# Two ordering edges in an interleaved attention and mixer kernel: the mixer's first loads and norm behind the attention's last steps, and the read-outs' denominators behind the row maxima of their step

## The chip, the cores and the metric

The kernel runs on one core of one Trainium2 chip. The metric is device time in microseconds (us) of one execution, so lower is better. One execution was also recorded by the hardware profiler; all rows of the profile and the trace come from that one.

## The reference

Four layers run one after the other on x, a sequence of S = 2048 rows with D = 640 columns: attention with a compressive memory, a gated mixer (gMLP), and both once more with the same weights.

```python
for i in range(2):
    x = x + A(layernorm(x))
    x = x + B(layernorm(x))

def A(x):                       # H = 32 heads of 20, N = 4 segments of 512 rows
    q, k, v = x @ wq, x @ wk, x @ wv        # per head and segment
    M, z = 0, 0
    for s in range(N):
        a_dot = softmax(q[s] @ k[s].T * 20**-0.5 + causal_mask) @ v[s]
        a_mem = (phi(q[s]) @ M) / (phi(q[s]) @ z + 1e-6)      # the memory's read-out
        o[s] = g * a_mem + (1 - g) * a_dot                    # g = sigmoid(beta), per head
        M += phi(k[s]).T @ v[s];  z += phi(k[s]).sum(rows)    # phi(t) = t + 1 if t > 0 else exp(t)
    return o @ wo

def B(x):
    z = gelu(x @ w_in)                      # 1728 columns: two halves of 864
    z1, z2 = z[:, :864], layernorm(z[:, 864:])
    return (z1 * (w_sp @ z2 + b_sp)) @ w_out
```

Products are made of fp16 parts: each operand is split into a high and a low half, and three matmuls (high by high, high by low, low by high) stand for one.

## The kernel before

**Stages.** Each attention is `phase1a` (class `Attention`, method `run`), each mixer is `phase1b` (output rows of the attention that are left, norm, product with w_in, gelu, norm of z2) and then `phase2` or `phase2s` (product with w_sp, gate, product with w_out). All in all: attention, mixer, attention, mixer.

**The attention's steps.** A segment has 16 pairs of heads, so there are N = 64 pairs in all four segments, and each pair takes three steps, c = 0, 1, 2. `run` counts steps t; pair n = t // 3 is the one whose exponentials are taken (`P`, L1276, on ScalarE). TensorE's order in this stage is the order of the program text (`manual_schedule` for PE); the other engines' order is made by a planner from priorities and from times that it simulates. In one step, in this order:

- `scores`: TensorE multiplies q by k for the row maxima of the pair two ahead (`mp`, L1267, then the mask, L1239), then k by q for the pair's own exponentials (`es`, the same lines). VectorE reduces `mp` to `mx` (L1283): 2 x 512 columns at c = 0, two blocks at c = 1, 2 x 256 at c = 2. ScalarE takes the exponentials.
- functions posted for this step by earlier ones (`post`, list `later`), the evictions of a read-out among them.
- `pvs` (L1320): 20 small matmuls for each head of a pair with `PH` and `PL`, the two halves of its exponentials, which ScalarE (L1293) and POOL (L1294; VectorE for some of the last four pairs) make.
- at c = 0, `maxes`: TensorE transposes the maxima of the next pair (`mtp`, L1301), ScalarE and VectorE split them (`mr`, L1303 and L1304), and two DMAs on the SP queue write them beside the pair's q (`qk<-mr`, L1306), where they act as the offset of the exponentials' argument.
- `until`: fill work for TensorE: the projections of q, k and v (`qps`, `kps`, `vps`), the output projection (`yps`, L1077) and, at steps given by a formula, a read-out.

**A read-out** is method `read`: for segments 1 to 3, and six of them per segment (five groups of heads, the last in two parts), TensorE multiplies phi(q) by the memory into `num` (L1163, L1167). Its function `out` is posted to the next step and has three VectorE instructions: `den` (L1172), its reciprocal (L1175) and the product `gm` (L1176). The read-out stands at the end of a step with c = 2, so `out` belongs to a step with c = 0. `num`, `mtp` and the products of a memory update (`mup`) are tiles of tag "ms" in pool `apm`, which has one buffer, one PSUM bank; the attention's PSUM pools use all eight banks, and `mp`, `es` and `pv` have one buffer each.

**Edges.** `tc.issue_after(i)` gives the instructions of its block that run on i's engine an edge: they are issued behind i. It adds no semaphore wait. `last_of` holds, for SP, ACT and DVE, the latest instruction of certain kinds: on SP a `qk` load or an `mr` DMA, on ACT an exponential or a v eviction, on DVE a row maximum `mx` or a v eviction. `hold` ties a block to all of them.

**The mixer's first tile.** `phase1b` goes over the 16 tiles of 128 rows in the order `ts`. Of tile 0 it loads the attention's result (`load`, L275), normalises it (`layernorm_stats`, L216 to L219, with POOL's power at L219; `xn`, L225), splits it (`xnhl`, L231 and L232) and transposes it by DMA into `th` (L233); TensorE then makes `zp` (L316) from `th` and w_in in two groups of 30 matmuls. The first such block, with the load of the second tile, stands in `tc.high_priority(offset=HP2)`, HP2 = 300:

```python
        with tc.high_priority(offset=HP2):
            a = load(ts[0])
            xn = attn_out(ts[0], *a)
            a = load(ts[1])
            th = xn_t(xn)
```

The rows that it loads (`x1_d`) are written in the course of the attention, the first of them long before its end, so nothing but buffers and priority holds the block back. In the trace its instructions stand at 616 to 635 us in the first attention's end, and at 1603 to 1617 and 1677 to 1688 us of the second, whose last row maximum is at 1802 us.

Of the kernel before, what the change touches and what calls it, by code (L numbers as in the profile page):

```python
# [2 lines left out]

# [32 lines left out]
HP2 = 300  # L36
# [209 lines left out]
NWO = 12  # L246


def phase1b(g, o_d, x, x1_d, z1_d, put, w0=None):
    nc, tc = g.nc, g.tc  # L250
    zs = ZS if w0 is None else ZB
    with ExitStack() as ctx:
# [50 lines left out]
        def xn_t(xn):  # L303
            th = pe2.tile([128, 2, KD, 128], F16, tag="th", name="th")
            hl = pe1.tile([128, 2, D], F16, tag="xnhl", name="xnhl")
            split_t(g, hl, th, xn)
            return th[:, 0], th[:, 1]
# [24 lines left out]

        g.mark = {}
        ts = [*range(NWO - 4), *range(NWO, NT), *range(NWO - 4, NWO)]
        with tc.high_priority(offset=HP2):
            a = load(ts[0])
            xn = attn_out(ts[0], *a)
            a = load(ts[1])
            th = xn_t(xn)
# [12 lines left out]
def whole(g, zh, zl):  # L352

    def put(t, z, pool):
        g.nc.scalar.copy(zh[:, t, :], z)
        g.nc.vector.tensor_tensor(zl[:, t, :], z, zh[:, t, :], ALU.subtract)

    return put


def blocks(g, zb):

    nc = g.nc
    even = {}

    def put(t, z, pool):
        j = t // 2
        l, r = z[:, :FHH], z[:, FHH:]

        def keep(b, src):  # L370
            nc.scalar.copy(zb[b][:, 0, j], src)
            nc.vector.tensor_tensor(zb[b][:, 1, j], src, zb[b][:, 0, j], ALU.subtract)

        def diff(a, b, nm):
            o = pool.tile([128, FHH], F32, tag=nm, name=nm)
            nc.gpsimd.tensor_tensor(o, a, b, ALU.subtract)
            return o

        if t % 2 == 0:
            keep(0, l)  # L380
            t1 = diff(r, l, "zt1")
            keep(3, t1)
            even[j] = r, t1
            return
        r0, t1 = even.pop(j)
        keep(1, l)
        keep(2, r)
        t2 = diff(r, t1, "zt2")
        keep(4, t2)
        keep(5, diff(r, r0, "zt3"))  # L390
        keep(6, diff(l, t2, "zt1"))

    return put
# [463 lines left out]
class Attention:  # L857
# [34 lines left out]
    def hold(self):  # L892
# [3 lines left out]
            held.enter_context(self.tc.issue_after(i))  # L896
        return held

    def soon(self, f):

        if self.now is None or self.now < 0:
            f()
        else:
            self.post(1, f)
# [240 lines left out]
    def read(self, s, m, c0):  # L1145

        g, nc = self.g, self.nc
        heads = UH[m]
        nh = len(heads)
        mst = self.mst[s % 2]  # L1150
        for i in range(max(m - 1, 0), m + 1):
            assert self.held["q", i] == s and self.held[s % 2, i] == s, (s, m, i, self.held)
        self.readout.add((s, m))
        if c0 == 0:
            self.gm[s, m] = self.pl2.tile([128, 4, 8, DH], F32, tag="gm", name="gm")
        gm = self.gm[s, m]
        n = min(6, nh - c0)
        f = heads[c0] - TH[m][0]
        low = [h for h in TH[m - 1] if h in heads[c0:c0 + n]] if m else []
        tp = self.pm.tile([128, L], F32, tag="ms", name="num")[:, :4 * n * (DH + 1)].rearrange("p (t h d) -> p t h d", t=4, h=n)  # L1160
        for t in range(4):
            c = slice(128 * t, 128 * t + 128)
            nc.tensor.matmul(tp[:, t], self.phq[m][:, c], mst[:, m, f:f + n, :], start=True, stop=not low,  # L1163
                             skip_group_check=True)
            if low:
                fl, nl = low[0] - TH[m - 1][0], len(low)
                nc.tensor.matmul(tp[:, t, :nl], self.phq[m - 1][:, c], mst[:, m - 1, fl:fl + nl, :],  # L1167
                                 start=False, stop=True, skip_group_check=True)

        def out():  # L1170
            den = self.u2.tile([128, 4, 6], F32, tag="den", name="den")[:, :, :n]
            nc.vector.scalar_tensor_tensor(den, tp[:, :, :, DH], g.epsd,  # L1172
                                           g.gate[:, heads[c0]:heads[c0] + n].unsqueeze(1).to_broadcast((128, 4, n)),
                                           ALU.add, ALU.mult)
            nc.vector.reciprocal(den, den)  # L1175
            nc.vector.tensor_tensor(gm[:, :, c0:c0 + n, :], tp[:, :, :, 0:DH],  # L1176
                                    den.unsqueeze(3).to_broadcast((128, 4, n, DH)), ALU.mult)

        self.post(1, out)

    def update(self, s, m, pk):

# [172 lines left out]
    def run(self, nseg=NSEG):  # L1355
        pairs = [(s, m, h0) for s in range(nseg) for m in range(NU) for h0 in UH[m][::2]]
        N = self.N = len(pairs)
# [42 lines left out]
        for c in order:  # L1400
            w = V if c[0] in "vp" else U
            beg = step(acc)
            if c[0] in "vp":
                i = int(c[1:])
# [9 lines left out]
            else:  # L1414
                s, m = int(c[0]), int(c[1])
                it = self.unit(s, m)
                i = NU * s + m - 4
# [39 lines left out]
        g = self.g  # L1457
# [14 lines left out]
            self.later[3 * i - LEAD + 2] = [lambda w=w: self.update(*w)]  # L1472
        for t in range(-LEAD, END):
            self.now = t
            f, c = divmod(t + self.LF, 3)
            if c == 0 and 0 <= f + self.LM < N:
                self.fetch(f + self.LM)
            p, r = divmod(t - self.LV - 2, 3)
            if r == 0 and 0 <= p < N:
                self.combine(p, *pairs[p])  # L1480
            n, c = divmod(t, 3)
            self.scores(n, c)
            for f in self.later.pop(t, ()):
                f()
            for h in range(2):
                p, r = divmod(t - self.LV - h, 3)
                if r == 0 and 0 <= p < N:
                    for _ in self.pvs(p, h, *pairs[p]):
                        pass
                if h == 1 and c == 0 and 0 <= n - 1 + self.LM < N:  # L1490
                    self.maxes(n - 1 + self.LM)
                if r == 0 and 0 <= p + 1 < N:
                    self.cast(p + 1, h)
            until(t + 1)
# [6 lines left out]
def phase1a(g, a, top, nseg=NSEG):  # L1501
    a.top = top
    with ExitStack() as ctx:
        a.setup(ctx)
        ctx.enter_context(g.tc.manual_schedule(engines=ENGINES))
        a.run(nseg)


@with_exitstack
def interleaved_layers(ctx, tc, x, wq, wk, wv, wo, beta, w_in, w_sp, b_sp, w_out, out):  # L1510
    nc = tc.nc
    g = Ctx()
    g.nc, g.tc = nc, tc
    cp = consts(g, ctx)
    g.bsp = cp.tile([128, NT], F32, tag="bsp", name="bsp")
    g.wpw = cp.tile([128, NT], F32, tag="wpw", name="wpw")
    g.wiv = cp.tile([128, NT], F32, tag="wiv", name="wiv")
    attn_consts(g, cp, beta)
    ats = ExitStack()
    attn_weights(g, ats, wv, wq, wk, wo, w_in, w_out)  # L1520

    def dram(name, shape, dt=F32):
        return nc.dram_tensor(name, shape, dt, kind="Internal").ap()

    def rows(a):
        return [a[0, t * 128:(t + 1) * 128, :] for t in range(NT)]

    g.st = [dram(f"st{i}", (D, 3, 2, L), F16) for i in range(2)]
    g.turned = [[dram(f"turned{t}_{i}", (128, 2048), F16) for i in range(2)] for t in range(NT)]
    kept = kept_tiles(g, ats)  # L1530
    xs = [rows(x), [dram(f"x2_{t}", (128, D)) for t in range(NT)], rows(out)]
    x1_d = [[dram(f"x1_{i}_{t}", (128, D)) for t in range(NT)] for i in range(2)]
    o_d = [[dram(f"o{i}_{n}", (L, 2, D), F16) for n in range(NSEG)] for i in range(2)]
    att = [Attention(g, xs[i], o_d[i], x1_d[i], kept) for i in range(2)]
    att[0].b_sp = b_sp
    for i in range(2):
        z1_d = [dram(f"z1_{i}_{t}", (128, FH)) for t in range(NT)]
        with ExitStack() as zs:
            with ExitStack() as top:
                phase1a(g, att[i], top)  # L1540
                if i:
                    ats.close()
                    w0 = zs.enter_context(tc.tile_pool(name="w0", bufs=1, reuse_waits="tile")).tile([128, 2, 7 * D], F16, name="w0")
                zp = zs.enter_context(tc.tile_pool(name="z2", bufs=1, reuse_waits="tile"))
                if i:
                    zb = [zp.tile([128, 2, NT // 2, FHH], F16, name=f"zb{j}") for j in range(7)]
                    phase1b(g, o_d[i], xs[i], x1_d[i], z1_d, blocks(g, zb), w0)
                else:
                    zh = zp.tile([128, NT, FH], F16, name="zh")
                    zl = zp.tile([128, NT, FH], F16, name="zl")  # L1550
                    phase1b(g, o_d[i], xs[i], x1_d[i], z1_d, whole(g, zh, zl))
            if i:
                phase2s(g, w_sp, x1_d[i], z1_d, zb, w0, xs[i + 1])
            else:
                phase2(g, w_sp, x1_d[i], z1_d, zh, zl, xs[i + 1], att[1])
# [26 lines left out]
```

## Time and profile before

| | us |
|---|---|
| runs (3), median | 2359.9 |
| runs, lowest and highest | 2358.45, 2361.67 |
| the profiled execution | 2362.26 |
| its span, first to last instruction | 2360.5 |
| first to last exponential of the first attention | 112.9 to 646.7 |
| first to last exponential of the second attention | 1314.4 to 1817.3 |
| mean granted TensorE clock | 0.977 |

The profiled execution lies 2.4 us above the median of the runs and 0.6 us above the slowest. In the profile PE is TensorE's matmul, PEld its weight load, DVE VectorE, ACT ScalarE, SP the queue that issues the DMAs. A row of the timeline has start, length, engine, line, operation, the tiles written and read, the shape, how many instructions are merged, and in brackets the idle time before it with what ended it. A row of stretches has the stretch, its length, the busy us of PE, PEld, DVE, ACT and POOL with the number of instructions, the granted clock (1.00 is full speed), the DMA engines' share and GB/s.

### The profile page before, as it was taken

To read this page: it belongs to the slowest core of one execution; us is meant where nothing else is said; L and a number is where in the kernel's file an instruction comes from. 1 tells how busy PE (TensorE), PEld (TensorE's weight loads), DVE (VectorE), ACT (ScalarE), POOL (GpSimd) and SP (SyncE) were. 2 spreads that over 40 slices of the span, in tenths; PEclk is the share of its full clock that TensorE was granted. 3 is DMA by queue.
4 is the path that set the end of the run, shared out by engine and by line. 5 is a ranking of instruction groups with operands and counts; after the bars stand their busy time and mean duration, and the time that the engine had idled before them with its cause. 6 is when DMAs were issued, how large, how long until landed. Compare 5 with 4: busy or idle time off the path is not lost. (4 is left out here: it accounts for less than half of the span.)

```text
span 2360.5 us, 50370 instructions
## 1 busy us (share of the span) xinstructions
PE 2184.8 (93%) x20490; PEld 1302.3 (55%) x20490; DVE 1503.1 (64%) x2790; ACT 1171.3 (50%) x1452; POOL 973.1 (41%) x726
## 2 busy tenths in 40 slices
PE   4778889899899999988998888999999999999998
PEld 2445555566645555555554555656566555555655
DVE  7578868777754543444533688787776668546454
ACT  3279678777732331111212697887776334322321
POOL 2078678888720100000001688888787323000000
PEclk9999899999999999999999999999999999999999
DMA  5553545555553457766665336454453634877885
GB/s 160 158 148 98 128 108 131 119 146 133 140 177 94 124 172 198 212 185 193 180 152 140 85 93 172 104 134 101 124 166 108 146 87 112 247 210 193 216 215 126
DMA packets 509416, 350.14 MB, mean 148 GB/s; under 512 B 409280, under 2 KB 444224, under 8 KB 504064
## 3 DMA queue, kind: packets, MB, share of 16 engines
q1 hardware_dynamic: 509184, 346.93, 55.7%
q8 instruction: 160, 2.62, 0.5%
q14 instruction: 72, 0.59, 0.1%
HBM read 160.83 MB, written 97.93 MB: 110 GB/s over the span
## 5 line engine op out<-in xcount | busy, mean ns | idle before, releaser
L1294 POOL TENSOR_TENSOR PL<-P,PH 128x1280 f16<-128x1280 f32 x248 | 649.9, 2622 | 121.8 <-ACT PH L1293 109.2
L1283 DVE TENSOR_REDUCE mx<-mp 128x2 f32<-128x1024 f32 (+3 forms) x512 | 408.9, 817 | 106.6 <-PE mp L1239 104.9
L1276 ACT ACTIVATE P<-es,sc 128x1024 f32<-128x1024 f32 (+1 forms) x384 | 370.4, 965 | 145.1 <-PE es L1239 142.6
L1293 ACT CAST PH<-P 128x1280 f16<-128x1280 f32 x256 | 320.4, 1253 | 19.8 <-PE pv L1320 11.5
L219 POOL TENSOR_TENSOR lnrs<-lnve,mhalf 128x1 f32<-128x1 f32 x92 | 56.6, 624 | 598.7 <-DVE lnve L218 595.4
L316 PEld LDWEIGHTS <-th 128*128 128x128 f16 x1920 | 188.1, 98 | 171.5 <-issue 8.6
L668 PE MATMUL gp<-zh,wt 128*128 128x432 f16 x1024 | 231.2, 346 | 0.0
L668 PEld LDWEIGHTS <-wt 128*128 128x128 f16 x1536 | 150.3, 98 | 128.9
L1267 PEld LDWEIGHTS <-qk 60*128 60x128 f16 (+1 forms) x2048 | 91.4, 94 | 227.8 <-issue 156.9
L469 PEld LDWEIGHTS <-wt 128*128 128x128 f16 x1344 | 131.5, 98 | 112.6
L1267 PE MATMUL mp<-qk 60*128 60x512 f16 (+3 forms) x1024 | 138.7, 308 | 40.2 <-DVE mx L1283 39.1
L1267 PE MATMUL es<-qk 64*128 64x512 f16 (+3 forms) x1024 | 136.2, 302 | 37.5 <-ACT P L1276 26.4
L1239 PEld LDWEIGHTS <-big 64*128 64x128 f16 x3072 | 142.0, 96 | 51.6 <-issue 4.9
L1320 PE MATMUL pv<-vs,PH 128*128 128x41 f16 x2560 | 167.9, 183 | 2.1 <-DVE ab L1336 2.0
L1044 PE MATMUL vps<-wvh,xt 128*128 128x320 f16 x640 | 155.1, 309 | 13.6 <-DMA xt<-xnhl 11.9
L1320 PE MATMUL pv<-vs,PL 128*128 128x41 f16 x2560 | 164.0, 182 | 1.6 <-POOL PL L1294 1.6
L1320 PEld LDWEIGHTS <-PH 128*128 128x128 f16 x2560 | 142.7, 96 | 18.8
L316 PE MATMUL zp<-wi1h,th 128*128 128x432 f16 x640 | 148.2, 346 | 0.6 <-DMA th<-xnhl 0.6
L1320 PEld LDWEIGHTS <-PL 128*128 128x128 f16 x2560 | 143.5, 97 | 4.3 <-POOL PL L1294 2.1
L668 PE MATMUL gp<-zl,wt 128*128 128x432 f16 x512 | 135.3, 346 | 0.0
L639 DVE TENSOR_REDUCE am<-wr 128x1 f32<-128x2048 f32 x16 | 36.5, 2284 | 152.1 <-DMA wr<-in_B_w_sp_dram 152.1
L1101 PE MATMUL kps<-xt,wkh 128*128 128x512 f16 x380 | 123.4, 394 | 6.2 <-DVE phl L1135 6.1
(248 smaller groups left out, 4384.6 us busy)
## 6 DMA issues: line engine op xcount, KB each, us to landing
wr<-in_B_w_sp_dram SPq DMA_DIRECT2D x32, 1024.0 KB
qk<-st SPq DMA_DIRECT2D x256, 120.0 KB
x<-x SPq DMA_DIRECT2D x56, 320.0 KB
z<-z SPq DMA_DIRECT2D x32, 432.0 KB
cz<-z SPq DMA_DIRECT2D x32, 432.0 KB
turned<-wt SPq DMA_DIRECT2D x24, 512.0 KB
wt<-turned SPq DMA_DIRECT2D x24, 512.0 KB
st<-qhl SPq DMA_DIRECT2D x40, 256.0 KB
```

The costliest lines, as they stand in the source:

```text
L316: nc.tensor.matmul(zp[:, n, :FHH], a[:, k, :], b[:, k, c:c + FHH], start=(k == 0 and j == 0), stop=(k == KD - 1 and j == 2))
L469: nc.tensor.matmul(o[:, :FHH], wt[:, x, m, :], zb[b][:, y, m, :], start=start and i == j == 0, stop=i == NP - 1 and j == 2, skip_group_che ...
L668: nc.tensor.matmul(gp[:, n, :FHH], ready[t][:, k % 2, a, k // 2, :], b[:, k, n * FHH:(n + 1) * FHH], start=(i == 0 and j == 0), stop=(i == ...
L1044: nc.tensor.matmul(ps, a[:, k, c], b[:, k, n * 320:(n + 1) * 320], start=(i == 0), stop=(i == 14))
L1101: nc.tensor.matmul(ps, a[:, k, c], b[:, k, :], start=(i == 0), stop=(i == 14))
L1239: nc.tensor.matmul(out, g.big[r, 64 - 64 * s:192 - 64 * s], mk, start=False, stop=s == 1, skip_group_check=True)
L1267: nc.tensor.matmul(out[:, h, o:o + w], a[r, ac], b[r, bc], start=o == 0, stop=False, skip_group_check=True)
L1276: self.last_of["ACT"] = nc.scalar.activation(P[:, :, 512 * c:512 * c + ew], es[:, :, :ew], AF.Exp, scale=g.esc).ins
L1283: self.last_of["DVE"] = nc.vector.tensor_reduce(self.mx[m][:, :, i], mp[:, :, o:o + w], AX.X, ALU.max).ins
L1293: nc.scalar.copy(PH, P[:, h])
L1294: (nc.gpsimd if h == 0 or n < self.N - self.TAIL else nc.vector).tensor_tensor(PL, P[:, h], PH, ALU.subtract)
L1320: nc.tensor.matmul(pv[:, i, h, :], x[:, c:c + 128], v[:, j, h0 + h, :], start=(j == 0 and x is PH), stop=(j == i and x is PL), skip_group_ ...
```

## The change

`phase1b` gets the context for its first block from outside: `Attention.ended`, which keeps the high priority and adds an edge to each instruction of `end_of`. That list is taken from `last_of` at the start of step 3N - 4 = 188: the last `mr` DMA on SP (step 186), the last row maximum on DVE (step 185) and the exponential of step 187 on ACT. And a read-out's `out` is wrapped in an edge to `last_of["DVE"]`: it runs in the step after the products, behind `scores`, so that this is the row maximum of that step.

```diff
-def phase1b(g, o_d, x, x1_d, z1_d, put, w0=None):
+def phase1b(g, o_d, x, x1_d, z1_d, put, first, w0=None):
...
         ts = [*range(NWO - 4), *range(NWO, NT), *range(NWO - 4, NWO)]
-        with tc.high_priority(offset=HP2):
+        with first:
             a = load(ts[0])
             xn = attn_out(ts[0], *a)
             a = load(ts[1])
...
+    @contextmanager
+    def ended(self):
+
+        with self.tc.high_priority(offset=HP2), ExitStack() as held:
+            for i in self.end_of:
+                held.enter_context(self.tc.issue_after(i))
+            yield
...
             nc.vector.tensor_tensor(gm[:, :, c0:c0 + n, :], tp[:, :, :, 0:DH],
                                     den.unsqueeze(3).to_broadcast((128, 4, n, DH)), ALU.mult)
 
-        self.post(1, out)
+        def held():
+            with self.tc.issue_after(self.last_of["DVE"]):
+                out()
+
+        self.post(1, held)
...
         for t in range(-LEAD, END):
             self.now = t
+            if t == 3 * N - 4:
+                self.first, self.end_of = self.ended(), [*self.last_of.values()]
...
-                    phase1b(g, o_d[i], xs[i], x1_d[i], z1_d, blocks(g, zb), w0)
+                    phase1b(g, o_d[i], xs[i], x1_d[i], z1_d, blocks(g, zb), att[i].first, w0)
...
-                    phase1b(g, o_d[i], xs[i], x1_d[i], z1_d, whole(g, zh, zl))
+                    phase1b(g, o_d[i], xs[i], x1_d[i], z1_d, whole(g, zh, zl), att[i].first)
```

More of the change, by code (lines that the diff above doesn't have):

```diff
@@ L1 @@
-from contextlib import ExitStack
+from contextlib import ExitStack, contextmanager
 from itertools import islice
```

## The prediction

> **What bounds the kernel now.** I read the page first, then stretches of equal work in both attentions, then single read-outs. Section 1 of the page gives busy time, share of the span and instructions of each engine:
>
> ```profile
> PE 2184.8 (93%) x20490; PEld 1302.3 (55%) x20490; DVE 1503.1 (64%) x2790; ACT 1171.3 (50%) x1452; POOL 973.1 (41%) x726
> ```
>
> TensorE leads, but the change touches only the two attentions, so their stages decide. In the view of stretches each row gives the length and the busy us of PE, PEld, DVE, ACT and POOL with instruction counts, then the granted clock, DMA share and GB/s. Rows come in pairs: the same steps of the first and of the second attention, cut at starts of the exponentials.
>
> ```profile
> 508.27:530.18 21.91, 21.66 (x301) 13.18 (x300) 16.30 (x34) 17.41 (x22) 18.47 (x13) 1.00 0.46 122
> 1672.87:1700.92 28.05, 24.61 (x301) 14.05 (x300) 20.37 (x40) 18.16 (x23) 19.03 (x14) 0.88 0.46 120
> 530.18:569.32 39.14, 39.12 (x537) 24.07 (x534) 28.68 (x58) 30.98 (x40) 33.15 (x22) 1.00 0.55 137
> 1700.92:1740.06 39.14, 39.11 (x537) 24.07 (x534) 28.67 (x58) 30.97 (x39) 33.15 (x22) 1.00 0.60 151
> 616.78:634.98 18.20, 13.94 (x211) 9.48 (x208) 15.79 (x32) 12.61 (x15) 12.51 (x11) 1.00 0.58 172
> 1789.81:1805.55 15.74, 13.66 (x211) 9.22 (x208) 10.86 (x20) 11.16 (x13) 12.24 (x9) 1.00 0.29 89
> ```
>
> Two things stand here. Undisturbed, the attention is TensorE's own pace (39.12 busy of 39.14). And lost time stays lost: the second attention loses 6.14 us in the second row (28.05 - 21.91), and the 39.14 us that follow are as long as in the first attention, where nothing had been lost. So a stall of TensorE is priced in full where it is saturated.
>
> **Part one: the denominators.** A read-out's products (`num`, on TensorE) end a step; its three VectorE operations (`den`, reciprocal, `gm`) belong to the next step. That next step always has c = 0, since read-outs stand at t = 2 (mod 3); it begins with `mp`, whose 1024 columns per partition VectorE reduces to `mx`, and after the pv products it has the transpose `mtp` of `maxes`. `num` and `mtp` share the one buffer of tag "ms". Here is a typical one, VectorE's timeline (start, length), then TensorE's:
>
> ```profile
> 537.80 0.24 DVE L1172 SCALAR_TENSOR_TENSOR den<-num,sc,gate 128x24 f32<-128x24 f32 x1 [1.89 <-PE num L1167]
> 538.07 0.30 DVE L1175 RECIPROCAL den<-den 128x24 f32<-128x24 f32 x1
> 538.48 0.66 DVE L1176 TENSOR_TENSOR gm<-num,den 128x480 f32<-128x480 f32 x1
> 539.05 1.22 DVE L1283 TENSOR_REDUCE mx<-mp 128x2 f32<-128x1024 f32 x1
> 540.19 0.68 DVE L1118 SCALAR_TENSOR_TENSOR qhl<-qps,qhl 128x512 f16<-128x512 f32 x1
> ```
>
> ```profile
> 538.35 0.25 PE L1239 MATMUL mp<-maskq,big 64*128 64x128 f16 x4
> ...
> 539.33 0.18 PE L1320 MATMUL pv<-vs,PL 128*128 128x41 f16 x1
> 539.35 0.27 PE L1301 MATMUL mtp<-ident,mx 128*8 128x128 f32 x1
> ```
>
> Today `gm` is done at 539.14, before `mtp` wants the buffer, and it lies beside `mp` on TensorE: it costs nothing. Behind `mx` that cover is gone, and `mtp` waits for it. That the dependency exists, and what it does when it bites, the trace shows. First the read-outs' tiles and `mtp`'s own row of semaphore waits, then the one place where `mtp` was late for it, and the delay from `mp` to `mx` on an idle VectorE:
>
> ```profile
> L1172 DVE SCALAR_TENSOR_TENSOR den<-num,sc,gate x36: 218/243/244, 224.5 to 1788.6; 128x24 f32<-128x24 f32 x30, 128x8 f32<-128x8 f32 x6
> ...
>   PE num L1167: 26.1, 15
>   PE num L1163: 7.8, 9
> who waited for it (us, times):
>   PE mtp L1301: 2.0, 2
> ```
>
> ```profile
> L1301 PEldq EVENT_SEMAPHORE  x36: 51/51/51, 225.8 to 1789.7; - x36
> ```
>
> ```profile
> 1680.21 0.89 DVE L216 BATCH_NORM_STATS2 lnst<-x 128x6 f32<-128x320 f32 x2 [2.31 <-DMA x<-x]
> ...
> 1682.12 0.66 DVE L1176 TENSOR_TENSOR gm<-num,den 128x480 f32<-128x480 f32 x1
> ```
>
> ```profile
> 1682.92 0.27 PE L1301 MATMUL mtp<-ident,mx 128*8 128x128 f32 x1 [1.57 <-DVE gm L1176]
> ```
>
> ```profile
> 1676.91 0.25 PE L1239 MATMUL mp<-maskq,big 64*128 64x128 f16 x4
> ```
>
> ```profile
> 1677.20 0.69 DVE L1283 TENSOR_REDUCE mx<-mp 128x2 f32<-128x512 f32 x1 [1.60 <-PE mp L1239]
> ```
>
> There are 36 read-outs, 30 wide and 6 narrow, and `mtp` carries 36 extra semaphore waits. The new moment of `mtp` at the typical place: `mp` ends at 538.60; `mx` starts 0.04 later (1677.20 against 1676.91 + 0.25); VectorE issues the next one 1.14 after that (539.05 to 540.19); `den` to the end of `gm` takes 1.34 (537.80 to 539.14); `mtp` follows 0.14 behind (1682.78 to 1682.92). Sum 2.66, so 541.26 instead of 539.35: **1.91 us of TensorE idle**. Queued behind `mtp` are the projection matmuls and the next step's `mp` and `es`, hence the exponentials. The narrow ones have a shorter chain:
>
> ```profile
> 615.60 0.23 DVE L1172 SCALAR_TENSOR_TENSOR den<-num,sc,gate 128x8 f32<-128x8 f32 x1 [0.86 <-PE num L1163]
> ...
> 616.42 1.23 DVE L1283 TENSOR_REDUCE mx<-mp 128x2 f32<-128x1024 f32 x1
> ```
>
> 0.82 in place of 1.34, so 1.39 us each. Before 24 of the 36 VectorE stood idle for `num` (15 + 9 above): it is free there, the typical case. At two thirds of each kind that is 20 x 1.91 + 4 x 1.39 = 43.8 us. At the other 12 VectorE comes late already, some of `mtp`'s wait exists, and the new part lies between 0 and 1.91; I take two thirds, 1.3 each, since only two of them show a wait of `mtp`: 15.6. Together **+59 us** (bounds 44 and 30 x 1.91 + 6 x 1.39 = 66). `mx` itself comes 0.41 earlier (538.64 for 539.05), worth nothing while `mtp` ends last.
>
> How much comes back later? Between the first and the last read-out of each attention TensorE is not saturated everywhere:
>
> ```profile
> 224.49:617.12 392.63, 360.75 (x4902) 231.67 (x4900) 303.99 (x596) 297.38 (x378) 314.67 (x217) 0.96 0.50 128
> 1415.55:1790.15 374.60, 352.77 (x4899) 225.55 (x4897) 293.01 (x583) 289.78 (x365) 314.16 (x219) 0.98 0.52 135
> ```
>
> Idle: 31.9 and 21.8, 54 us. Waits for an engine with a backlog would shrink when that engine gets 1.9 us to catch up; round trips through one buffer would not. I take a seventh: **-8** (0 to -27).
>
> **The clock.** The next rows are stretches of 3.41 us, cut where the granted clock changes, each with the one after it:
>
> ```profile
> 1321.62:1325.03 3.41, 1.63 (x21) 1.08 (x21) 2.32 (x6) 2.90 (x5) 3.41 (x2) 1.00 0.99 127
> 1325.03:1328.44 3.41, 3.41 (x56) 2.53 (x55) 1.87 (x7) 1.79 (x3) 2.15 (x2) 1.00 0.27 73
> 1680.02:1683.43 3.41, 1.59 (x29) 1.14 (x30) 3.02 (x8) 1.11 (x1) 1.83 (x2) 1.00 0.16 47
> 1683.43:1686.84 3.41, 2.04 (x10) 0.77 (x10) 3.38 (x5) 1.73 (x2) 1.30 (x1) 0.51 0.00 0
> ```
>
> Idle of 1.78 in a stretch left the clock at 1.00, idle of 1.82 was followed by 0.51. A wide stall leaves TensorE idle from 539.51 (end of pv) to 541.26, 1.75 us: just under, and over it with any other gap in the same stretch. If stretches run on regardless of the work, a stall lies wholly in one with chance (3.41 - 1.75) / 3.41 = 0.49; I let half of those reach the limit: 30 x 0.49 / 2 = 7, each costing half of 3.41: **+12** (0 to 61, all 36). [...]
>
> **Part two: loads and norm of phase1b's first tile.** The norm that now stands in the second attention's middle blocks VectorE on a load (the 2.31 at 1680.21); moved to the end, its 6.14 us go. In the first attention it costs 18.20 - 15.74 = 2.46. A second such norm lies in the second attention; between 0 and 6.14, I take 1, since one load was seen blocking. **-9.6**.
>
> What it costs at the end: moved are two loads on SP and, of the first tile, two statistics, aggregate and variance on VectorE, POOL's power, `xn`, ScalarE's copy, VectorE's low half and the transposing DMA; the second tile follows its load. SP must first issue the last `mr`, VectorE the last `mx`, ScalarE an exponential. Queued behind the statistics are then `rs`, `ab` and the PL subtractions of the last pairs, for which the pv products wait: a load waited for there like the one of 2.31 is in the upper bound.
>
> ```profile
> 1677.30 0.34 SPq L275 DMA_DIRECT2D x<-x  x1
> ...
> 1687.24 1.37 SPq L233 DMA_TRANSPOSE th<-xnhl  x1
> ```
>
> ```profile
> 1809.88 0.50 SPq L1306 DMA_DIRECT2D qk<-mr  x1
> ```
>
> ```profile
> 1824.92 0.17 DVE L1331 TENSOR_TENSOR rs<-pv,iomg 128x8 f32<-128x8 f32 x1 [1.59 <-PE pv L1320]
> ```
>
> ```profile
> 1827.49 7.00 PE L316 MATMUL zp<-w,th 128*128 128x432 f16 x30 [2.62 <-DVE ab L1336]
> ```
>
> The load goes out at 1810.4; the transposing DMA follows a load by 9.9 us (1677.30 to 1687.24) and issues for 1.4: `th` is there at about 1822 or later, and the first `zp` group can stand behind the last pv products (1824.9) instead of before them. A group takes up to 7.0, so the second group starts near 1831 instead of 1827.5; TensorE no longer waits for `ab`, which gives some back. I take 3.5 for both attentions (0 to 10). **Part two: -6** (-10 to +4).
>
> **Sum:** 59 - 8 + 12 - 6 = +57. The profiled execution took 2362.3 us (span 2360.5); the median of the runs is 2359.9. From the median: **2417**. How the planner reorders other queues no trace of before shows; I allow 6 us either way.
>
> **Rivals.** [...] (2) Every stall halves it: 59 - 8 + 61 - 6 = +106, 2466. For it: 0.51 after 1.82; against: stalls cut by a border. (3) Half of the stalls is taken back where TensorE idles anyway: 59 / 2 - 6 = +24, 2384. For it: 54 us of idle; against: 39.12 of 39.14. (4) The other side: the stall is covered. Place: the step behind each read-out; if `mp` there waits for `mx` and not for TensorE's own work, the chain through `mx` paces it, and 0.41 earlier gives 30 x 0.41 = 12 us: -12 - 6, 2342. It decides from the point where TensorE has over 1.91 us idle behind each read-out; the saturated rows say it has 0.02 in 39.14. (5) The tie changes nothing, because VectorE's order comes out as before: -6, 2354; the `last_of` of that step is the `mx` of its own c = 0, so I see no way to it but an oversight.
>
> **Numbers.** Forecast 0.48, (1) 0.20, (2) 0.10, (3) 0.11, (4) 0.06, (5) 0.04, no change 0.01. What this kernel's measurement can tell from no change is about 0.2%, 4.7 us. Faster: (4) and (5), 0.10; same 0.01; slower 0.89. The range 2378 to 2442 holds the forecast with its bounds, (1), most of (3) and the lower part of (2); outside are (4), (5) and some 0.08.
>
> **What would show it.** Right: `mtp` waiting for `gm` some 30 times, 45 to 65 us in all; `mx` ahead of `den` at every read-out; the pair at 1672.87 as long as its twin plus one stall; stretches at granted clock 0.5 behind some stalls; no norm of phase1b in the second attention's middle. Wrong: those waits absent, or present while the steps' lengths stay.

## The result and the profile after

The changed kernel takes **2446.4 us** (median of 4 runs, 2445.05 to 2448.38) against 2360.8 us (4 runs, 2358.45 to 2362.92) for the kernel before on the same chip: a ratio of 1.0371, 95% interval 1.0355 to 1.0387, or +85.6 us. Forecast were +57 and a range up to 2442. The sign and the mechanism hold; the size does not, and rows show which terms were too small. The profiled execution took 2445.05 us (span 2443.3).

TensorE's semaphore waits in the trace of the changed kernel (us in total, times, longest):

```profile
PE mtp L1313 <- DVE gm L1184: 71.9, 36, 4.5
PE zp L316 <- DMA th<-xnhl: 7.4, 3, 3.6
```

The first row stood at 2.0 us and 2 times before. All 36 read-outs now hold `mtp`. The second row stood at 0.6 us and once before; its growth belongs to part two.

The stretches of the prediction, at the same steps, in the changed kernel; the last two rows are the steps t = 45 to 186 of the two attentions:

```profile
522.56:546.77 24.21, 21.71 (x300) 13.08 (x299) 16.16 (x33) 17.71 (x23) 18.50 (x13) 1.00 0.40 110
1737.88:1762.10 24.22, 21.73 (x301) 13.10 (x299) 16.18 (x33) 17.72 (x22) 18.50 (x13) 1.00 0.39 108
546.77:597.64 50.87, 43.59 (x534) 25.46 (x531) 28.41 (x58) 31.41 (x39) 33.33 (x23) 0.90 0.41 106
1762.10:1812.45 50.35, 43.57 (x541) 25.47 (x537) 28.55 (x58) 31.33 (x39) 33.09 (x22) 0.90 0.50 140
223.33:668.87 445.54, 385.01 (x5077) 241.39 (x5074) 313.01 (x615) 311.43 (x389) 326.36 (x225) 0.94 0.44 115
1454.05:1881.62 427.57, 375.41 (x5075) 236.90 (x5072) 293.83 (x590) 302.46 (x375) 322.62 (x225) 0.96 0.44 116
```

The same steps before:

```profile
225.74:634.98 409.24, 373.10 (x5078) 240.24 (x5075) 318.30 (x625) 309.17 (x391) 326.15 (x227) 0.96 0.51 130
1416.80:1805.55 388.75, 364.84 (x5075) 233.85 (x5072) 302.39 (x600) 300.12 (x376) 325.36 (x227) 0.98 0.51 133
```

Three things are to be seen. The norm is gone from the second attention's middle: 28.05 and 21.91 us have become 24.22 and 24.21. The saturated stretch of 39.14 us has become 50.87, and only part of that is idle: TensorE's idle there is 50.87 - 43.59 = 7.3 us, but its *busy* time has grown from 39.12 to 43.59 for the same matmuls, at a granted clock of 0.90. Over all these steps the time grows by 75.1 us: idle from 60.1 to 112.7 (+52.6), busy from 737.9 to 760.4 (+22.5). Nearly all of the busy part is the clock, as the records of the clock show below.

**The typical stall** came out as worked out. VectorE, then TensorE, in the changed kernel:

```profile
613.04 1.23 DVE L1295 TENSOR_REDUCE mx<-mp 128x2 f32<-128x1024 f32 x1 [2.73 <-PE mp L1251]
614.18 0.23 DVE L1180 SCALAR_TENSOR_TENSOR den<-num,sc,gate 128x24 f32<-128x24 f32 x1
...
614.45 0.30 DVE L1183 RECIPROCAL den<-den 128x24 f32<-128x24 f32 x1
...
614.85 0.66 DVE L1184 TENSOR_TENSOR gm<-num,den 128x480 f32<-128x480 f32 x1
```

```profile
612.74 0.25 PE L1251 MATMUL mp<-maskq,big 64*128 64x128 f16 x4
615.66 0.27 PE L1313 MATMUL mtp<-ident,mx 128*8 128x128 f32 x1 [1.76 <-DVE gm L1184]
```

`mtp` starts 2.67 us behind the end of `mp` (forecast 2.66), and TensorE stood idle for 1.76 (forecast 1.75). **The long ones** were not foreseen:

```profile
556.37 0.23 DVE L1180 SCALAR_TENSOR_TENSOR den<-num,sc,gate 128x24 f32<-128x24 f32 x1
556.52 0.68 DVE L1126 SCALAR_TENSOR_TENSOR qhl<-qps,qhl 128x512 f16<-128x512 f32 x1
557.12 0.75 DVE L1131 TENSOR_SCALAR qps<-qps,sc 128x512 f32<-128x512 f32 x1
...
557.85 0.29 DVE L1183 RECIPROCAL den<-den 128x24 f32<-128x24 f32 x1
558.06 0.65 DVE L1133 SCALAR_TENSOR_TENSOR phq<-eq,sc,qps 128x512 f32<-128x512 f32 x1
...
558.74 0.60 DVE L1184 TENSOR_TENSOR gm<-num,den 128x480 f32<-128x480 f32 x1
```

Between `den` and `gm` the planner has put three evictions of a projection. The chain takes 2.97 us instead of 1.33, and `mtp` waits 3.40. Five read-outs have evictions there (3.38 to 4.50 us of idle); five more have 1.84 to 2.62, four of them because a norm's `xt` stands between `mx` and `den`. The edge holds `out` back behind `mx`, but nothing holds the rest of VectorE's work behind `out`.

**The clock.** Two pairs of stretches of 3.41 us in the changed kernel. In the first the stall, from 530.36 to 532.12, is cut by the border; in the second, from 613.90 to 615.66, it lies whole in one stretch:

```profile
527.63:531.05 3.42, 2.73 (x43) 1.88 (x42) 1.55 (x4) 2.58 (x4) 3.07 (x3) 1.00 0.27 76
531.05:534.46 3.41, 2.34 (x23) 1.20 (x24) 2.18 (x6) 2.54 (x5) 2.95 (x2) 1.00 0.00 1
612.97:616.38 3.41, 1.65 (x34) 1.25 (x29) 2.95 (x8) 2.58 (x4) 3.35 (x3) 1.00 0.35 74
616.38:619.79 3.41, 3.41 (x25) 1.73 (x24) 2.01 (x4) 1.11 (x1) 2.86 (x3) 0.51 0.25 42
```

The same idle of 1.76 us costs nothing more in the first place, and in the second a stretch at half clock follows. The trace also keeps its own records of the granted clock, with start and length. By them the steps t = 45 to 186 hold 8 runs at half clock before (44 us) and 23 after (87 us). TensorE was busy for 41.6 us of the former and 81.1 us of the latter; half of that is lost (the matmuls that were busy for 39.12 us at a clock of 1.00 were busy for 43.59 at 0.90, and 39.12 / 0.90 = 43.5), 20.8 and 40.5 us, so the clock accounts for 19.7 of the 75.1 us, about a quarter. All changes of the clock on record in the changed kernel lie within 0.01 us of one grid of 3.413 us, though the work differs from step to step. The grid's borders are some 0.1 us later than the cuts of the rows above.

**The attention's end**, second attention, changed kernel: SP, VectorE, ScalarE's last exponential, TensorE's first `zp`.

```profile
1885.98 0.50 SPq L1318 DMA_DIRECT2D qk<-mr  x1
1886.54 0.86 SPq L275 DMA_DIRECT2D x<-x  x2
...
1900.36 1.35 SPq L233 DMA_TRANSPOSE th<-xnhl  x1
```

```profile
1878.38 0.67 DVE L1295 TENSOR_REDUCE mx<-mp 128x2 f32<-128x512 f32 x1
1889.57 0.89 DVE L216 BATCH_NORM_STATS2 lnst<-x 128x6 f32<-128x320 f32 x2 [0.65 <-DMA x<-x]
1895.75 3.57 DVE L1306 TENSOR_TENSOR PL<-P,PH 128x1280 f16<-128x1280 f32 x1
1899.24 1.09 DVE L232 TENSOR_TENSOR xnhl<-xn,xnhl 128x640 f16<-128x640 f32 x1
```

```profile
1892.04 0.69 ACT L1288 ACTIVATE P<-es,sc 128x512 f32<-128x512 f32 x1 [0.46 <-PE es L1251]
```

```profile
1903.81 0.90 PE L316 MATMUL zp<-wi1h,th 128*128 128x432 f16 x2 [3.58 <-DMA th<-xnhl]
```

The load goes out directly behind the last `mr`; the norm starts 11.2 us behind the last `mx`; a subtraction of 3.57 us stands ahead of `xnhl`; `zp`, which waits for `th`, starts 3.45 us behind the issue of `th`. `zp` begins 11.8 us behind the start of the last exponential; in the kernel before it began 0.95 behind it.

### The profile page after: what moved, and what is told of

Read it like the earlier page. It is cut to its first block, busy times and chain, and to the rows that moved or that the text cites. A ratio compares the mean times of both kernels' runs of the same rounds, so it can differ in the third digit from the quotient of the medians.

```text
span 2443.3 us, 50376 instructions
## 1 busy us (share of the span) xinstructions
PE 2207.0 (90%) x20490; PEld 1306.7 (53%) x20490; DVE 1497.5 (61%) x2790; ACT 1179.0 (48%) x1452; POOL 972.8 (40%) x726
## 5 line engine op out<-in xcount | busy, mean ns | idle before, releaser
L1305 ACT CAST PH<-P 128x1280 f16<-128x1280 f32 x256 | 320.5, 1253 | 19.0 <-PE pv L1332 10.2
L1052 PE MATMUL vps<-wvh,xt 128*128 128x320 f16 x640 | 159.1, 316 | 13.8 <-DMA xt<-xnhl 11.9
```

The costliest lines, as they stand in the source:

```text
L1052: nc.tensor.matmul(ps, a[:, k, c], b[:, k, n * 320:(n + 1) * 320], start=(i == 0), stop=(i == 14))
L1305: nc.scalar.copy(PH, P[:, h])
```

## The experiments

Each time is set against runs of the kernel before on the same chip, so differences are to those.

| run | median us | against before | ratio, 95% interval |
|---|---|---|---|
| the change | 2446.4 | +85.6 | 1.0371 (1.0355 to 1.0387) |
| part two alone | 2357.8 | -0.3 | 0.9996 (0.9983 to 1.0008) |
| part one alone | 2448.9 | +90.8 | 1.0389 (1.0364 to 1.0414) |
| part one, `mtp` in pv's bank | 2408.8 | +50.7 | 1.0217 (1.0196 to 1.0238) |
| before, `mtp` in pv's bank | 2402.3 | +44.4 | 1.0191 (1.0175 to 1.0207) |
| part one, TensorE kept busy | 2432.7 | +74.7 | 1.0308 (1.0283 to 1.0333) |
| change, 4 matmuls in the stall | 2432.1 | +75.7 | 1.0321 (1.0298 to 1.0345) |
| change, other work behind `gm` | 2435.5 | +77.6 | 1.0330 (1.0314 to 1.0346) |
| change, `den` times 1.0 | 2507.3 | +149.5 | 1.0628 (1.0610 to 1.0646) |
| change, `gm` twice | 2511.3 | +155.0 | 1.0659 (1.0632 to 1.0685) |
| part two, loads and norm freed earlier | 2352.0 | -5.9 | 0.9974 (0.9963 to 0.9986) |
| part two, loads untied | 2348.8 | -10.1 | 0.9963 (0.9949 to 0.9976) |
| part two, tie at 3N - 16 | 2354.7 | -4.2 | 0.9982 (0.9966 to 0.9997) |

**Which part.** Each part was put alone into the kernel before (`with first:` and `ended`; the `held` wrapper).

> Part two alone (the tie of phase1b's first loads and norm), the read-outs as before. Theory: in the attentions it gives back about 9 us (6 in the second, 2.5 in the first, 1 for the other tile), at the two ends it costs about 12 (th comes late): 2364 us, between 2358 and 2368. Rival: the ends cost what they cost only because the read-outs upset the planner's order, and the part alone gains: 2352 to 2356.

> Part one alone (denominators behind the row maxima), phase1b's first block as before. Theory: 36 waits of mtp for gm, about 70 us in all, and more half-clock stretches: 2440 us, between 2432 and 2450. Rival: most of the loss is the end of the attentions and the planner's order: under 2420.

Part one alone came as its theory said. It is the whole loss and 5 us more: there a norm of `phase1b` meets a read-out, and one `mtp` waits 6.58 us. Part two alone is not told from no change; its 2357.8 us lies between the ranges of its theory and of the rival. Its steps t = 45 to 186, then those of part one alone:

```profile
226.41:631.78 405.37, 372.30 (x5078) 239.36 (x5075) 312.23 (x613) 307.77 (x389) 325.76 (x225) 0.97 0.50 127
1415.30:1797.67 382.37, 362.39 (x5075) 233.09 (x5072) 296.38 (x588) 298.97 (x374) 323.00 (x225) 0.99 0.48 130
```

```profile
223.78:673.49 449.71, 382.86 (x5078) 240.09 (x5075) 315.94 (x627) 312.64 (x391) 327.23 (x227) 0.94 0.45 118
1451.82:1890.85 439.03, 379.19 (x5075) 239.43 (x5072) 304.25 (x602) 304.40 (x377) 325.15 (x227) 0.95 0.44 118
```

Part two gains 3.9 + 6.4 = 10.3 us in these steps and loses as much at the ends. Part one adds 66.6 us of idle and 24.1 us of busy time; `mtp`'s wait grew by 76.7 - 2.0 = 74.7, so 8 us of the stalls came back in other waits. By the records of the clock, half speed costs 43.2 us there, 22.4 more than in the kernel before.

**Is it the buffer that `mtp` shares with `num`?** `mtp` was moved into the unused columns of pv's bank, with part one and, as a control, without it. `self.bank` is the bank of the pv tile; the first `mtp`, ahead of any pv tile, stays where it was:

```diff
-        tp = self.pm.tile([128, 512], F32, tag="ms", name="mtp")[:8, :128]
+        if self.pv:
+            tp = self.bank[:8, 384:512]
+        else:
+            tp = self.pm.tile([128, 512], F32, tag="ms", name="mtp")[:8, :128]
...
```

> As the run with part one alone, but mtp is written into the unused columns 384 to 511 of the pv tile's bank, so it no longer shares a buffer with num. The order of den behind mx stays. Theory (the wait of mtp for gm is the whole cost): no wait of mtp for gm, 2355 to 2368 us. Rival (the later denominators cost VectorE or POOL time by themselves, or the planner's order does): over 2390.

> The kernel before with one edit: mtp is written into the last 128 columns of the bank of pv instead of a buffer of tag ms; nothing is ordered behind mx. Control for the run with both. Theory A (in that run the denominators' order cost nothing any more, and what was left of its +48 us, 2408.8 against about 2360, is the wait of pv for the reader of the shared bank): this kernel alone comes to 2400 to 2410, with a wait of pv for ab of about 50 us at about 50 places, and the steps t = 45 to 186 of both attentions as long as in that run within 4 us. Theory B (the order itself costs even where mtp has its own bank): this kernel stays within 10 us of before, 2360 to 2370. Anything between divides the +48.

The first came out some 40 us above its theory: over 2390, as the rival had said, but not for the rival's reason. `mtp`'s waits for `gm` are gone, and a wait of pv for `ab` has come, with part one and then without:

```profile
PE pv L1327 <- DVE ab L1343: 53.2, 52, 3.9
```

```profile
PE pv L1323 <- DVE ab L1339: 51.8, 51, 3.4
```

The control carries the same wait and +44.4 of the +50.7 us, as its theory A said; but the steps t = 45 to 186 of the two runs lie 8.6 us apart (826.0 and 817.4), not within 4. The ratios differ by 0.0026, and the half-widths of their intervals are 0.0021 and 0.0016, so what the order costs without the shared buffer is some 6 us, at the edge of what can be told from zero. Next to the +90.8 of part one that is little: its loss is the wait for `num`'s buffer. One reserve remains: both runs stall at pv instead, and a cost of the order that those stalls cover would not be seen.

**How much is the clock?** Unread matmuls of 184 columns were put ahead of `mtp` behind each read-out, 14 of them with part one alone, 4 with the whole change (4 leave the typical idle at 1.44 us). The edit with 14; `fw` is a weight:

```diff
+                    if t - 1 in self.rd:
+                        fw = self.g.w["q"][0]
+                        for _ in range(14):
+                            self.nc.tensor.matmul(self.bank[:, 328:512], fw[:, 0, 0:128], fw[:, 0, 0:184],
+                                                  start=True, stop=True, skip_group_check=True)
```

> As the run with part one alone, but 14 matmuls of 184 columns whose result nobody reads stand before mtp in each step behind a read-out (about 1.1 us of TensorE work into unused columns of the pv bank), so that the stall is as long but TensorE is idle for under 0.7 us of it in most places. Theory (the clock is a part of the price): few half-clock stretches, 10 to 18 us less than part one alone, 2422 to 2432. Rival (the stall alone, clock not worth 5 us): within 5 us of part one alone.

> The changed kernel with four unread matmuls of 184 columns (about 0.35 us of TensorE) ahead of mtp behind each read-out: the chain on VectorE and the moment of mtp stay as they are, TensorE's idle of the typical stall falls from 1.76 to about 1.4 us. The four take TensorE time that was idle before. Theory A (the clock halves behind a stretch that holds about 1.75 us of idle or more, not behind less): the typical stalls no longer halve it, 8 of about 23 half-clock stretches go, -14 us, and some of the long ones' too; time 2428 to 2436, no half-clock stretch behind a stall of 1.4 us. Theory B (the loss by the clock falls in proportion to the idle, a fifth): -5 us, 2440 to 2443. Theory C (the clock was no part of the price): 2445 to 2449.

Work that nobody needs makes the kernel faster: by 16.2 us with 14 (against part one alone), by 9.9 with 4 (against the change; 14.3 by the medians). By the records of the clock, half speed costs 22.5 instead of 43.2 us with 14 (11 runs for 24) and 26.2 instead of 40.5 with 4 (15 for 23). A stall in the run with 4 that lies whole in one stretch, and the stretch behind it:

```profile
1678.84:1682.25 3.41, 1.97 (x37) 1.39 (x31) 2.99 (x8) 3.02 (x5) 3.35 (x3) 1.00 0.32 72
1682.25:1685.66 3.41, 3.41 (x50) 2.27 (x49) 2.00 (x4) 1.91 (x4) 3.19 (x3) 1.00 0.02 6
```

With 1.44 us of idle in the stretch, the next stays at 1.00. Of the 22 stalls with 1.3 to 1.52 us in that run none is followed by half clock; in the changed kernel 8 of the 18 with 1.73 to 1.80 are. The step between 1.44 and 1.76 is what theory A said, and the time fell into its bounds; set against the kernel before, the gain of 9.9 is short of its 14.

**Does a us on the chain cost a us?** Shortening it: the read-out's `out` first in its step, and the step's other posted functions behind its `gm` (`gm_ins`):

```diff
...
         self.post(1, held)
+        self.later[self.now + 1].remove(held)
+        self.later[self.now + 1].insert(0, held)
...
-            for f in self.later.pop(t, ()):
-                f()
+            for i, f in enumerate(self.later.pop(t, ())):
+                with self.tc.issue_after(self.gm_ins) if i and t - 1 in self.rd else ExitStack():
+                    f()
```

> The changed kernel; a step's read-out is issued first in the step after, and the other posted operations of that step are ordered behind its gm, so that less other VectorE work (qhl, qps, wol, phl) gets between den and gm. Theory A (slip-ins between mx and gm made part of the stall, 1.3 to 2.8 us each at five places, and a price of 1:1): the wait of mtp for gm falls from 71.9 to about 62 to 66 us, the mean of one from 2.0 to 1.75, and the time by 6 to 9 us to 2437 to 2441, a little lower if the half-clock stretches get fewer too. Theory B (VectorE's other work is only moved to the next wait): same time as the changed kernel, 2444 to 2449.

```profile
PE mtp L1315 <- DVE gm L1184: 64.1, 36, 3.4
```

The wait fell by 7.8 and the time by 8.0 us (against before; 10.9 by the medians). Of the five read-outs with evictions in the chain two are left. This looks like the price of 1:1 of theory A, but it is not. The steps t = 45 to 186 of this run:

```profile
223.44:666.54 443.10, 381.88 (x5078) 240.54 (x5075) 311.15 (x615) 311.38 (x389) 326.77 (x225) 0.94 0.46 116
1452.31:1872.27 419.96, 368.85 (x5075) 234.96 (x5072) 292.51 (x590) 302.69 (x375) 323.09 (x225) 0.98 0.45 119
```

Against the changed kernel these steps are 10.1 us shorter, but by the two profiles TensorE's idle is as long as without the edit: 112.3 for 112.7 us. What `mtp` no longer waits, other matmuls wait (`es` for `P` 17.1 us instead of 10.2, `vps` for `phl` 3.1 instead of 0). That part is what theory B said. The gain is in the busy time, 9.7 us less, and the records of the clock have 16 runs at half clock instead of 23, which cost 30.2 instead of 40.5 us. That the time fell by as much as the wait is a coincidence.

Lengthening the chain, by `nc.vector.tensor_scalar(den, den, 1.0, None, ALU.mult)`, which stands behind the reciprocal and not ahead of it as the expectation has it, and by a second, equal `gm`:

> The changed kernel with one more VectorE operation in the chain at all 36 read-outs: den is multiplied by 1.0 between the sum and the reciprocal (128x24 or 128x32, a quarter to a third of a us). Theory A (each us on the chain from mx to gm is a us of TensorE's and so of the time, with the clock's loss on top): 36 x 0.25 to 0.35 = +9 to +13 us of stall, the wait of mtp for gm 81 to 86 us, and the time 2455 to 2464. Theory B (the attention takes it back in the steps behind a read-out): under +5 us, 2444 to 2451.

> The changed kernel with the read-outs' last operation made twice: gm is written a second time with the same values, 0.58 us from issue to issue for the 30 wide read-outs and 0.3 for the 6 narrow ones, an operation whose length other engines' work does not stretch in the traces so far. Theory A (a us on the chain is a us of TensorE's idle, and a stretch of 3.41 us that holds about 1.75 us of idle is followed by one at half clock, which costs 1.7): 30 x 0.58 + 6 x 0.3 = +19 us of stall; a typical stall of 2.34 us has a piece of 1.75 or more in one stretch with chance 0.67, one of 1.76 us with 0.49, so 5 half-clock stretches more, +9 us; time 2474 (2468 to 2480). Theory B (stall alone): 2465. Theory C (the attention takes it back): under 2450.

Both forecasts failed by a factor, each first through the price of the operation. The multiplication, which I had put at a quarter of a us, in the groups of its tile (ns min, median, max), and its longest instance on VectorE beside GpSimd's timeline:

```profile
L1184 DVE TENSOR_SCALAR den<-den x36: 164/568/2333, 227.3 to 1925.3; 128x24 f32<-128x24 f32 x30, 128x8 f32<-128x8 f32 x6
```

```profile
616.06 2.33 DVE L1184 TENSOR_SCALAR den<-den 128x24 f32<-128x24 f32 x1
```

```profile
615.76 2.60 POOL L1307 TENSOR_TENSOR PL<-P,PH 128x1280 f16<-128x1280 f32 x1 [0.62 <-ACT PH L1306]
```

It ends 0.03 us behind GpSimd's running instruction. The second `gm` costs 0.98 us at most of the wide read-outs instead of 0.58: it starts 0.32 us behind the end of the first. So the waits grew to

```profile
PE mtp L1314 <- DVE gm L1185: 111.0, 36, 6.1
```

and, in the other run, to

```profile
PE mtp L1315 <- DVE gm L1186: 105.3, 36, 5.5
```

that is by 39.1 and 33.4, and against the change's own +85.6 us the times grew by 63.9 and 69.4. More than the stall itself is lost each time: runs at half clock go from 23 to 31 and 33, which cost 17.8 and 26.5 us more, and TensorE's idle in the steps t = 45 to 186 grows by 45.0 and 40.2. Nothing of the kind that the attention would take back is to be seen in these two runs.

**Where part two loses its gain.** Three forms of it, all without part one. First both the loads untied and the norm's edge earlier; then only the loads untied, with the edge at 3N - 4 as it was; then the loads untied and the edge earlier still, at 3N - 16. The first, against the changed kernel:

```diff
+        with tc.high_priority(offset=HP2):
+            a0, a = load(ts[0]), load(ts[1])
         with first:
-            a = load(ts[0])
-            xn = attn_out(ts[0], *a)
-            a = load(ts[1])
+            xn = attn_out(ts[0], *a0)
...
-        self.post(1, held)
+        self.post(1, out)
...
-            if t == 3 * N - 4:
+            if t == 3 * N - 10:
```

> The kernel before with another form of part two: the Mixer's first two loads stay untied, as in before, and only the norm is ordered behind the last steps, behind the engines' work of 3N - 10 instead of 3N - 4. Theory A (part two alone gained 10 us in the attentions and lost 10 at the attention's ends, because the loads, the x1 subtraction and the transposing DMA stood in a row behind the tie): the gain in the attentions stays at 7 to 10 us, the end of each attention is as before within 2 us, so 2348 to 2353, a ratio to before of 0.995 to 0.998. Theory B (what the norm takes from the attention it takes wherever it stands): within 0.2% of before, 2356 to 2362.

> The kernel before with part two of which one piece is undone: the Mixer's first two loads are untied as in before, and the norm stays ordered behind the engines' work of 3N - 4. Theory A (of the 10 us that part two loses at the attentions' ends, the loads are a third: their DMA, 3 us from issue to the norm's first operation, stood in the row): the attentions as in part two alone (527 to 531 and 494 to 499 us from the first to the last exponential), the end of each attention (last exponential to the second group of zp) 2 to 4 us shorter than in part two alone, and the time 2351 to 2355. Theory B (the row is that of the norm, the x1 subtraction and the transposing DMA; the loads lie beside the last steps): the ends as in part two alone, 2356 to 2360.

> As the run with loads early and the norm ordered behind the engines' work of 3N - 10, but of 3N - 16: the norm's VectorE work comes about 8 row maxima earlier in the second attention. Theory A (only what the norm did in the middle of the attention cost, and any tie near the end takes that away): 2350 to 2354, like the run with 3N - 10, ends as in before. Theory B (the norm costs again as soon as it has steps of the attention behind it): half of the gain gone, 2354 to 2358, the attentions 2 to 5 us longer than with 3N - 10.

All three beat the kernel before, and the one with the loads alone untied is the fastest kernel here, 2348.8 us. Its second attention's end (VectorE, SP, the last exponential, `zp`):

```profile
1790.05 0.67 DVE L1291 TENSOR_REDUCE mx<-mp 128x2 f32<-128x512 f32 x1
1790.65 1.65 DVE L216 BATCH_NORM_STATS2 lnst<-x 128x6 f32<-128x320 f32 x4
```

```profile
1799.95 1.55 SPq L233 DMA_TRANSPOSE th<-xnhl  x1
```

```profile
1804.70 0.68 ACT L1284 ACTIVATE P<-es,sc 128x512 f32<-128x512 f32 x1
```

```profile
1805.06 0.53 PE L316 MATMUL zp<-wi1h,th 128*128 128x432 f16 x2
```

From start to start, the norm follows the last `mx` by 0.6 us instead of 11.2, and `zp` the last exponential by 0.36 us instead of 11.8 (11.7 in part two alone). Theory A had given the loads a third of the loss; they are nearly all of it, and both theories' times were too high. The runs with the edge at 3N - 10 and 3N - 16 have ends like those of before, but keep 9.5 and 5.8 us of the attentions' gain (first to last exponential) against 12.2; that is theory A for 3N - 10 and theory B for 3N - 16. The three times lie within 6 us of each other, and between 3N - 4 and 3N - 10 the intervals do not settle the order.

## Why the prediction was wrong in size

- **Stalls, +59: measured 69.9** (71.9 - 2.0). The typical one was right to 0.01 us. Two steps failed. The one gave the 12 read-outs at which VectorE "comes late already" only 1.3 us each, 15.6 in all: in the changed kernel they wait 21.9 us, of which 2.0 stood there before, 1.8 us each. The other took no other VectorE work into the chain: the remaining 24 wait 50.0 us instead of 43.8, seven of them long ones with 22.5 us. Together that is the missing 11. It would be 5 more in like units: the sum counts `mtp`'s delay, 1.91, and not the 1.75 of idle that its own section on the clock has, and the trace counts idle.
- **Give-back, -8: right in size.** Part one alone: 74.7 of stalls, 66.6 of idle. The wait that shrank most is that of `es` for `P` (15.8 to 10.4 us), an engine that catches up, as was argued; but the seventh itself was taken without a row, so that the size fits is luck. Half taken back (rival 3) and the covered stall (rival 4) are out, and so is a tie without effect (rival 5).
- **Clock, +12: measured 16 to 22.** 22.4 us by the records of the clock in part one alone and 19.7 in the change, 16.2 us by the run with 14 matmuls. The forecast rightly took stretches as running on regardless (the changes on record lie on one grid of 3.413 us), with a chance of 0.49 that a stall lies whole in one, and then halved it: "I let half of those reach the limit" (by the recorded grid the two stretches that it took the limit from hold 1.71 and 1.76 us of idle, not 1.78 and 1.82). That halving is the step that failed: 8 of 18 typical stalls were followed by half clock (0.44), and all ten long ones. Halving everywhere (rival 2) is out: the other ten typical stalls, each cut by a border of the grid, were followed by the full clock. A clock that costs nothing (rival 1: 59 - 8 - 6 = +45, 2405) is out as well: gaps of 1.76 us were followed by half clock, and half speed costs 40.5 us in the changed kernel instead of 20.8.
- **Part two, -6: measured -0.3 alone.** The gain of 9.6 us in the attentions was right (10.3). The cost at the ends, 3.5 with a bound of 10, was some 11 in the profile of part two alone (its span grew by 0.8 although the steps lost 10.3). I had dated the load rightly, behind the last `mr`. The step that failed is the chain behind it: from the load to the issue of `th` it took 13.8 us and not 9.9, with a subtraction of 3.57 ahead of `xnhl`, and from there to `zp` 3.45 and not the 1.4 of the issue alone. The run with the loads untied shows that the tie of the loads is what put this chain behind the last exponential.
- **The sum:** 70 for 59, 16 to 22 for 12, nothing for -6, with the give-back of -8 as forecast: 78 to 84, where the medians differ by 85.6 and the two profiled spans by 82.8. The range failed at its upper end, 2442: it took the stalls at 66 at most and gave the cases with many half-clock stretches too small a share.

The signs named in advance held: `mtp` waited for `gm` (36 times, but 71.9 us and not 45 to 65), `mx` stood ahead of `den` everywhere, the stretch at 1672.87 became as long as its twin, 24.2 us, which is the twin of before and a stall of 2.3, half-clock stretches appeared behind some stalls, and the norm left the second attention's middle.

## What to carry to other kernels

Before an operation is ordered behind another on a shared engine, ask which buffer it releases and who waits for that, and add to the chain whatever else the engine may slip in. Price a stall of the matmul engine twice, once for its length and once for the clock: idle of 1.76 us, about half a stretch of 3.41, bought a stretch at half speed here where it lay whole in one, and useless matmuls in the gap can be cheaper than the gap (14 behind each read-out made part one alone 16.2 us faster). And a wait that falls is not yet time gained: look at which other waits grow. When work is tied to the end of a stage, tie the computation and not its loads: with the loads in the tie the gain of 10 us was lost again, without it the kernel became 0.4% faster than before.

## What was not expected of the hardware

- Among the 36 stalls of the changed kernel the clock's limit shows sharply. By the longest piece of idle inside one stretch of the recorded grid, none of the 17 up to 1.61 us was followed by half clock and all 16 with 1.76 us or more were; of the three between, two were. Over all traces it is a band and not a number. In the changed kernel a stretch with 1.26 us of idle was followed by half clock:

```profile
316.10:319.52 3.42, 2.16 (x42) 1.98 (x39) 2.37 (x3) 3.30 (x6) 2.41 (x3) 1.00 0.34 79
319.52:322.93 3.41, 3.41 (x23) 2.10 (x22) 0.45 (x1) 0.76 (x1) 3.35 (x2) 0.50 0.38 95
```

In part one alone a stretch with 2.10 us (80.60 to 84.01) was not, and in the run with 4 matmuls one stall with 1.81 us inside one stretch was not. What else decides is not shown.
- In the run with `den` times 1.0 the in-place `TENSOR_SCALAR` on 128x24 took 0.16 to 2.33 us: where it took 0.3 or more it ended 0.03 to 0.04 us behind a GpSimd instruction that was running at its start (the longest at 618.39, GpSimd's at 618.36), and where none ran it took 0.16 to 0.18 (0.18 at 260.18, with GpSimd idle until 260.67). The reciprocal of the same tile took 0.30 at the median and 0.304 at most. Why it ends with GpSimd's instruction no trace shows.
